# LSH attention with a fused feed-forward network: an add by transfer, features behind the product, an earlier load, one engine per last output

## The chip, the cores and the metric

The program runs on one core of one Trainium2 chip, in one launch. The metric is the device time of that launch in microseconds (us). The engines are TensorE (PE, matmuls and transposes), VectorE (DVE), ScalarE (ACT), GpSimd (POOL), and SyncE (SP), which here only issues transfers.

## The reference

Attention first: 4 batches, 8 heads, 768 tokens of 64 numbers. Each query and key is hashed to 6 bits, the signs of its products with a projection; a query sees only keys with equal bits. Then a feed-forward network (FFN) over all 3072 tokens.

```python
mask = q_bucket[:, :, :, None] == k_bucket[:, :, None, :]
scores = np.where(mask, scale * (q @ k.T), -1e9)       # per batch and head
attn = np.exp(scores - scores.max(-1, keepdims=True))
attn = attn / (attn.sum(-1, keepdims=True) + 1e-09)
x = (attn @ v).transpose(0, 2, 1, 3).reshape(B * S, H * D)   # 3072 x 512
h = x @ w_in                                           # 512 -> 2048
g = h * np.clip(h + 3.0, 0.0, 6.0) / 6.0
out = g @ w_out                                        # 2048 -> 512
```

## The kernel before

All inputs and outputs are fp32; a matrix product is done as three matmuls of numbers split in a high and a low half (names with h and l at the end: xh, xl, gh, gl, ph, pl). ScalarE makes most high halves by a cast, DVE or POOL the low ones by a subtraction.

**Attention** is a loop over 192 steps k, one for each 128 queries of a head: the transposes pt of the weights (L351), the accumulation acc of the values (L388, L389; 12 matmuls in every second step, for 256 queries), the scores s of a later step (L319, L322). DVE takes the minimum (L329) and makes pl (L375), ScalarE the exponential (L341) and ph (L374). ScalarE copies a finished acc to y (L416). One half of its partitions holds the product of the high values, the other that of the low ones. SP stores the one half in an HBM buffer xs, and POOL adds the other there by an accumulating transfer (`add()`, L395), one of 512 columns and one of 256 for every head. In the last head of a batch (`last_head`) DVE adds the two halves instead (L413, L414), and SP's store is enough.

**FFN.** Batch 0's FFN runs in the middle, after step 52. Those of batches 1 to 3 are a generator, `ffn()`, which the attention loop resumes twice per step, so that its matmuls lie between those of the attention; when the attention is over, it runs on alone. It works on chunks of 256 tokens, three per batch, called the first to the ninth here (h1_0 to h3_2), and in each on 16 blocks fc of 128 hidden features: gemm1 (12 matmuls into h, L494 to L496), a yield, gemm2 of the block before (6 matmuls into po, L516 to L518), the gate (ScalarE L503, DVE L504, gh, and gl on POOL, L509), a yield.

**Features of the next chunk** are made on the side. `begin()` loads xr from xs and puts small jobs in a list `side`: some empty ones, one that inverts the sums (L434, L435), one that spreads them to a tile rb (L442, POOL), and one for each of four feature blocks that transposes rb to rt on PE (L452), multiplies it in on DVE (L455) and spreads the next. `beside()` takes one job off the list. It is called once behind the gate and once more after the yield, just before the next gemm1. When the list is empty, `split()` makes xh on ScalarE (L485), and xl on DVE for feature blocks 0 and 2, on POOL for 1 and 3 (L486). In the last batch tiles of the tags kk and qq take their place.

**Order.** The instruction order of PE, DVE, ScalarE and POOL is that of the program text; each engine runs its own list in order. `bank()` hands out four PSUM banks, two of each of the tags pt and pu, which alternate: pt, acc, rt and h all come from it. SP and POOL issue their transfers in order.

Of the kernel before, what the change touches and what calls it, by code (L numbers as in the profile page):

```python
# [33 lines left out]
WA = 4  # L34
WB = 5
XE = 8
XF = (9, 8)
NWARM = 30


# [1 line left out]
def lsh_attention_moe(  # L42
# [10 lines left out]
    nc = tc.nc  # L53
    B, H, D, S = qkT.shape
    D //= 2
    DM, DF = w_in.shape
# [17 lines left out]
    def dma(out: bass.AP, in_: bass.AP):  # L74
        nonlocal last
        last = nc.sync.dma_start(out=out, in_=in_)
# [3 lines left out]
    def bank(shape, name: str, tag: str | None = None):  # L80

        nonlocal turn
        if tag is None:
            tag = ("pt", "pu")[turn % 2]
            turn += 1
        return ps.tile(shape, F32, name=name, tag=tag, bufs=2)
# [311 lines left out]
    def output(un: int):  # L398
        nonlocal vdone
        i, u = divmod(un, KT // 2)  # L400
        b, h = divmod(i, H)
        o = (h % 2) * D
        acc = accs.pop(un)

        if u != 1:
            outs[i] = sp.tile([P, 4 * P if u == 0 else 2 * P], F32, name=f"y{i}_{u}", tag=f"y{u}", bufs=1)
        y = outs[i][:, 2 * P :] if u == 1 else outs[i][:, : 2 * P]

        r = slice(o, o + D)
        r2 = slice(D - o, 2 * D - o)  # L410
        last_head = h == H - 1
        if last_head:
            nc.scalar.copy(y[r], acc[r2])  # L413
            nc.vector.tensor_add(y[r], acc[r], y[r])  # L414
        else:
            nc.scalar.copy(y, acc[:])  # L416
        if u:
            c = slice(0, 4 * P) if u == 1 else slice(4 * P, S)
            to = xs[b][h * D : (h + 1) * D, c]

            with tc.issue_after(copied.ins):
                dma(out=to, in_=outs[i][r])
            if not last_head:
                adds.append((i, to, outs[i][r2]))
        vdone = 2 * un + 2
# [31 lines left out]
    def load_x(b: int, t: int, ccs: range):  # L457
        assert all(not b * H <= a[0] < b * H + ccs.stop * P // D for a in adds)
        ts = slice(t * TC, (t + 1) * TC)
        xr = sp.tile([P, NCC, TC], F32, name=f"xr{b}_{t}", tag="ob")  # L460
        dma(
            out=xr[:, : len(ccs)], in_=xs[b][: len(ccs) * P, ts].rearrange("(cc p) t -> p cc t", p=P)
        )
        return xr

    def scale_x(b: int, t: int, ccs: range, xr, rc=None):

        name = f"{b}_{t}"
        rbs = {}

        def invert():
            rbs["rc"] = rc if rc is not None else inverse(name, b, slice(t * TC, (t + 1) * TC), ccs)

        def spread_next(cc: int):
            if cc < len(ccs):
                rbs[cc] = spread(name, rbs["rc"], cc)

        def then(cc: int):
            normalise(f"{name}_{cc}", xr[:, cc], rbs.pop(cc), "pt" if ffn_on and b == 0 else None)
            spread_next(cc + 1)  # L480

        return [invert, lambda: spread_next(0)] + [lambda cc=cc: then(cc) for cc in ccs]

    def split_x(x, src, engine):
        nc.scalar.copy(x[0], src)  # L485
        engine.tensor_sub(x[1], src, x[0].bitcast(F32))  # L486

    def gemm1(n: str, fc: int, x, tag: str | None = None):
        hp = bank([P, TC], f"h{n}_{fc}", tag)
        wi = wt[2 * fc]  # L490
        for cc in range(NCC):
            xh, xl = x[cc]
            wc = slice(cc * P, (cc + 1) * P)
            nc.tensor.matmul(hp[:], lhsT=wi[:, 0, wc], rhs=xh, start=(cc == 0), stop=False)  # L494
            nc.tensor.matmul(hp[:], lhsT=wi[:, 0, wc], rhs=xl, start=False, stop=False)  # L495
            nc.tensor.matmul(hp[:], lhsT=wi[:, 1, wc], rhs=xh, start=False, stop=(cc == NCC - 1))  # L496
        return hp
# [22 lines left out]
    def store(b: int, t: int, po, end: bool = False):  # L520
        ob = sp.tile([P, TC // P, DM], F32, name=f"ob{b}_{t}", tag="ob")
        r0 = b * S + t * TC
        to = out[r0 : r0 + TC, :].rearrange("(u p) d -> p u d", p=P)
        for u in range(TC // P):
            if end:

                x = DM // 2
                nc.scalar.mul(ob[:, u, :x], po[u][:, :x], 1.0 / 6.0)
                nc.vector.tensor_scalar_mul(ob[:, u, x:], po[u][:, x:], 1.0 / 6.0)
                dma(out=to[:, u], in_=ob[:, u])  # L530
            else:
                nc.scalar.mul(ob[:, u], po[u], 1.0 / 6.0)
        if not end:
            dma(out=to, in_=ob[:])
# [4 lines left out]
    side = []  # L539

    def beside():
        if side:
            side.pop(0)()
# [185 lines left out]
    def ffn():  # L729
        nonlocal ffn_on  # L730
        chunks = [(b, t) for b in range(1, B) for t in range(NTC)]
        xr, xhl = {}, {}
        pend = None

        def there(c: int) -> bool:

            return vdone >= (chunks[c][0] + 1) * HK

        def begin(c: int):
            b, t = chunks[c]  # L740
            xr[c] = load_x(b, t, range(NCC))
            todo = scale_x(b, t, range(NCC), xr[c])
            if b < B - 1:
                side.extend([lambda: None] * 2 + todo)
                return

            side.extend([lambda: None] * (4 if t else 6) + todo[:2])
            for cc in range(NCC):
                side.append(todo[2 + cc])
                side.append(lambda cc=cc: (place(c) if cc == 0 else None, split(c, cc)))  # L750

        def place(c: int):
            b, t = chunks[c]
            n = f"{b}_{t}"
            if b == B - 1 and t % 2 == 0:
                h, l = (
                    sp.tile([P, 2 * S], F32R, name=f"{x}{n}", tag=x)[:, : NCC * TC] for x in ("kk", "qq")
                )
                h, l = (x.rearrange("p (cc t) -> p cc t", cc=NCC) for x in (h, l))
            else:  # L760
                h, l = (sp.tile([P, NCC, TC], F32R, name=f"{x}{n}", tag=x, bufs=1) for x in ("xh", "xl"))
            xhl[c] = [(h[:, cc], l[:, cc]) for cc in range(NCC)]

        def split(c: int, cc: int):
            split_x(xhl[c][cc], xr[c][:, cc], (nc.vector, nc.gpsimd)[cc % 2])

        def finish():
            nonlocal pend
            which, (fc, po, gh, gl) = pend
            gemm2(fc, po, gh, gl)  # L770
            pend = None
            if fc + 1 < NFC:
                return lambda: None
            return lambda: store(*which, po, which == chunks[-1])

        for c, (b, t) in enumerate(chunks):
            while not there(c):
                if pend is not None:
                    finish()()
                yield  # L780
            n = f"{b}_{t}"
            if c not in xr:
                begin(c)
            while side:
                beside()
                yield
                yield
            if c not in xhl:
                place(c)
                for cc in range(NCC):  # L790
                    split(c, cc)
            ffn_on = True
            copy, engine = (nc.scalar.copy, nc.vector) if b == B - 1 else (nc.vector.tensor_copy, nc.gpsimd)
            po = None
            for fc in range(NFC):
                hp = gemm1(n, fc, xhl[c])
                yield
                end = finish() if pend is not None else lambda: None
                if po is None:
                    po = ps.tile([P, 2, 512], F32, name=f"po{n}", tag="s" if b == B - 1 and t % 2 == 0 else "po", bufs=1)  # L800
                gg = gate(n, fc, hp, copy, engine)
                end()
                pend = ((b, t), (fc, [po[:, u] for u in range(2)], *gg))
                if c + 1 < len(chunks) and c + 1 not in xr and there(c + 1):
                    if fc >= XF[chunks[c + 1][0] == B - 1]:
                        begin(c + 1)
                if fc + 1 == NFC and c + 1 in xr and c + 1 not in xhl and not side:
                    place(c + 1)
                    for cc in range(NCC):
                        split(c + 1, cc)  # L810
                else:
                    beside()
                yield
                beside()
            del xhl[c]
        finish()()

# [182 lines left out]
```

## Time and profile before

| what | value |
|---|---|
| time, median of 3 runs | 1032.8 us (1032.73 to 1034.37) |
| profiled execution | 1033.77 us |
| its span, first to last instruction | 1031.6 us |
| TensorE clock granted, mean | 0.995 of full speed (the 2.4 GHz level) |
| busy: PE, DVE, ScalarE, POOL | 98%, 67%, 57%, 46% of the span |

The profile is that of one execution. Spans of matmuls overlap in it, since their ends are modelled; the distance from one start to the next tells more. In brackets behind a row of the timeline stands how long the engine was idle before it, and what released it.

### The profile page before, as it was taken

How to read it: one execution, taken by the hardware profiler on the slowest of the kernel's cores; microseconds unless marked ns; L12 is line 12 of the kernel's file. 1: busy time of each engine (PE TensorE's matmuls, PEld its weight loads, DVE VectorE, ACT ScalarE, POOL GpSimd, SP SyncE). 2: the span in 40 equal slices, each digit the busy share in tenths (PEclk: the TensorE clock that was granted, in tenths of full speed). 3: DMA queues.
4: the chain of work that ended last, by engine and by line, in shares of the span. 5: the costliest groups of instructions: out<-in, count | busy, mean ns of one | idle time of the engine just before them, and what ended most of it. 6: DMA issues, size and time to landing. Idle time of an engine off the chain costs nothing.

```text
span 1031.6 us, 19001 instructions
## 1 busy us (share of the span) xinstructions
PE 1007.9 (98%) x6846; PEld 925.8 (90%) x6846; DVE 688.2 (67%) x1445; ACT 585.2 (57%) x1311; POOL 470.4 (46%) x522
## 2 busy tenths in 40 slices
PE   8999989999999999999999999999999999999998
PEld 7999878888899998898999999999999999899996
DVE  6999988889579999656556666655656553333332
ACT  6889865555488887544544554554455452333332
POOL 5677625566357775634553534553544232200100
PEclk9999999999999999999999999999999999999999
DMA  3566669000145555322321322221232010101000
GB/s 102 149 139 178 169 213 352 2 1 1 26 135 114 119 125 133 69 62 52 95 48 40 84 71 56 64 77 41 63 95 44 20 32 29 42 1 42 1 22 20
DMA packets 47412, 80.68 MB, mean 78 GB/s; under 512 B 5924, under 2 KB 27812, under 8 KB 47320
## 3 DMA queue, kind: packets, MB, share of 16 engines
q1 hardware_dynamic: 42840, 73.98, 24.5%
q0 software_dynamic: 4480, 5.51, 4.8%
q8 instruction: 54, 0.88, 0.4%
q14 instruction: 38, 0.31, 0.1%
HBM read 41.95 MB, written 18.09 MB: 58 GB/s over the span
## 4 chain that ended last, share of the span: by engine, by line
PE 80%; DVE 12%; ACT 3%; issue 3%; DMA 1%; POOL 0%; DVEq 0%; POOLq 0%; ACTq 0%
PE pt L351 10%; PE h L495 7%; PE h L494 7%; PE h L496 7%; PE po L516 7%; PE po L518 7%; PE po L517 7%; PE acc L388 6%; PE acc L389 6%; PE s L319 5%; PE s L322 5%; DVE pl L375 2%; DVE p L329 2%; DVE qq L290 1%; PE z L281 1%
## 5 line engine op out<-in xcount | busy, mean ns | idle before, releaser
L329 DVE TENSOR_SCALAR_CACHE_REDUCE p<-s 128x768 f32<-128x768 f32 x192 | 183.5, 955 | 99.8 <-PE pt L351 95.4
L375 DVE TENSOR_TENSOR pl<-pt,ph 128x384 fp32r<-128x384 f32 x376 | 191.7, 550 | 50.7 <-ACT ph L374 48.9
L374 ACT CAST ph<-pt 128x384 fp32r<-128x384 f32 x376 | 165.5, 481 | 53.4 <-PE pt L351 42.6
L341 ACT ACTIVATE p<-p,m 128x768 f32<-128x768 f32 x192 | 179.6, 935 | 9.3 <-DVE p L329 8.8
L503 ACT ACTIVATE g<-h,three 128x256 f32<-128x256 f32 x192 | 91.4, 476 | 153.5 <-PE h L496 129.5
L351 PE MATMUL pt<-ident,p 128*128 128x128 f32 x1152 | 161.5, 274 | 7.3 <-DVE pl L375 5.7
L509 POOL TENSOR_TENSOR gl<-g,gh 128x256 fp32r<-128x256 f32 x96 | 74.4, 775 | 202.9 <-DVE gh L508 159.8
L351 PEld LDWEIGHTS pt<-ident,p 128*128 128x128 f32 x1152 | 136.5, 141 | 25.6 <-PE pt L351 4.0
L504 DVE SCALAR_TENSOR_TENSOR g<-g,h 128x256 f32<-128x256 f32 x192 | 80.5, 419 | 114.1 <-ACT g L503 111.7
L388 PE MATMUL acc<-ph,vv 128*128 128x256 f32 x564 | 152.6, 303 | 3.1 <-DVE pl L375 3.1
L494 PE MATMUL h<-xh,w 128*128 128x256 f32 x512 | 147.8, 289 | 1.2 <-ACT y L416 1.2
L495 PE MATMUL h<-xl,w 128*128 128x256 f32 x512 | 143.3, 280 | 0.1
L496 PE MATMUL h<-xh,w 128*128 128x256 f32 x512 | 143.2, 280 | 0.0
L389 PE MATMUL acc<-pl,vv 128*128 128x256 f32 x564 | 141.0, 283 | 0.0
L516 PE MATMUL po<-w,gh 128*128 128x512 f32 x320 | 126.7, 396 | 0.1
L518 PE MATMUL po<-w,gl 128*128 128x512 f32 x320 | 126.6, 395 | 0.0
L517 PE MATMUL po<-w,gh 128*128 128x512 f32 x320 | 126.2, 394 | 0.0
L388 PEld LDWEIGHTS acc<-ph,vv 128*128 128x128 f32 x564 | 107.3, 190 | 6.2 <-DVE pl L375 1.9
L389 PEld LDWEIGHTS acc<-pl,vv 128*128 128x128 f32 x564 | 107.8, 191 | 0.0
L319 PE MATMUL s<-kk,qq 76*128 76x384 f32 x384 | 101.6, 345 | 2.2 <-ACT kk L295 1.5
L322 PE MATMUL s<-kk,qq 128*128 128x384 f32 x384 | 100.6, 343 | 0.0
L494 PEld LDWEIGHTS h<-xh,w 128*128 128x128 f32 x512 | 96.4, 188 | 3.8 <-ACT y L416 2.4
(136 smaller groups left out, 2019.3 us busy)
## 6 DMA issues: line engine op xcount, KB each, us to landing
raw<-in_qkT SPq DMA_DIRECT2D x32, 384.0 KB, 3.5
kk<-qq SPq DMA_DIRECT2D x62, 192.0 KB, 3.2
wr<-in_w_in SPq DMA_DIRECT2D x16, 512.0 KB, 9.7
wr<-in_w_out SPq DMA_DIRECT2D x16, 512.0 KB
vr<-in_v SPq DMA_DIRECT2D x32, 192.0 KB, 2.8
qq<-qq SPq DMA_DIRECT2D x31, 192.0 KB, 3.6
out<-ob SPq DMA_DIRECT2D x11, 512.0 KB, 3.0
xr<-xs SPq DMA_DIRECT2D x9, 512.0 KB
```

The source lines that it names most:

```text
L329: nc.vector.tensor_scalar(out=pr_[:], in0=s[:, :, :HW], scalar1=CAP, scalar2=None, op0=ALU.min, op1=ALU.min, accum_out=m[:],)
L341: nc.scalar.activation(pr_[:], pr_[:], AF.Exp, bias=m[:], scale=-1.0, accum_out=sms[b][:, t, h : h + 1])
L351: nc.tensor.transpose(pt[:, x], probs[g][0][:, c, x * P : (x + 1) * P], ident[:])
L375: nc.vector.tensor_sub(lo[:, :, w], pt[:], hi[:, :, w].bitcast(F32))
L388: nc.tensor.matmul(acc[:], lhsT=vv[:, kt], rhs=hi[:, x], start=(kt == 0), stop=False)
L389: nc.tensor.matmul(acc[:], lhsT=vv[:, kt], rhs=lo[:, x], start=False, stop=(kt == KT - 1))
L494: nc.tensor.matmul(hp[:], lhsT=wi[:, 0, wc], rhs=xh, start=(cc == 0), stop=False)
L495: nc.tensor.matmul(hp[:], lhsT=wi[:, 0, wc], rhs=xl, start=False, stop=False)
L496: nc.tensor.matmul(hp[:], lhsT=wi[:, 1, wc], rhs=xh, start=False, stop=(cc == NCC - 1))
L516: nc.tensor.matmul(po[u], lhsT=gh[:, us], rhs=wo[:, 0], start=(fc == 0), stop=False)
L517: nc.tensor.matmul(po[u], lhsT=gh[:, us], rhs=wo[:, 1], start=False, stop=False)
L518: nc.tensor.matmul(po[u], lhsT=gl[:, us], rhs=wo[:, 0], start=False, stop=(fc == NFC - 1))
```

## The change

Five edits. In batch 1, the last head's first 512 columns are stored and added by transfer as in other heads, and only its last 256 are added on DVE. The chunks of the last batch are begun from block fc 7 on instead of 8. The list of the first chunk has three empty jobs instead of two. The second call of `beside()` stands directly behind gemm1 instead of before the next one, and not in block 0. Of the last output, ScalarE scales all 512 columns for the first 128 tokens and DVE all 512 for the others, where each did half of both.

```diff
@@ -34,7 +34,7 @@
 WA = 4
 WB = 5
 XE = 8
-XF = (9, 8)
+XF = (9, 7)
 NWARM = 30
 
 
@@ -408,7 +408,8 @@
 
         r = slice(o, o + D)
         r2 = slice(D - o, 2 * D - o)
-        last_head = h == H - 1
+
+        last_head = h == H - 1 and (b != 1 or u == 2)
         if last_head:
             nc.scalar.copy(y[r], acc[r2])
             nc.vector.tensor_add(y[r], acc[r], y[r])
@@ -524,9 +525,10 @@
         for u in range(TC // P):
             if end:
 
-                x = DM // 2
-                nc.scalar.mul(ob[:, u, :x], po[u][:, :x], 1.0 / 6.0)
-                nc.vector.tensor_scalar_mul(ob[:, u, x:], po[u][:, x:], 1.0 / 6.0)
+                if u == 0:
+                    nc.scalar.mul(ob[:, u], po[u], 1.0 / 6.0)
+                else:
+                    nc.vector.tensor_scalar_mul(ob[:, u], po[u], 1.0 / 6.0)
                 dma(out=to[:, u], in_=ob[:, u])
             else:
                 nc.scalar.mul(ob[:, u], po[u], 1.0 / 6.0)
@@ -741,7 +743,7 @@
             xr[c] = load_x(b, t, range(NCC))
             todo = scale_x(b, t, range(NCC), xr[c])
             if b < B - 1:
-                side.extend([lambda: None] * 2 + todo)
+                side.extend([lambda: None] * (2 if c else 3) + todo)
                 return
 
             side.extend([lambda: None] * (4 if t else 6) + todo[:2])
@@ -794,6 +796,8 @@
             po = None
             for fc in range(NFC):
                 hp = gemm1(n, fc, xhl[c])
+                if fc:
+                    beside()
                 yield
                 end = finish() if pend is not None else lambda: None
                 if po is None:
@@ -811,7 +815,6 @@
                 else:
                     beside()
                 yield
-                beside()
             del xhl[c]
         finish()()
 
```

How the edits move instructions is shown in three places. On PE, in block 12 of the first chunk (h1_0), where a feature block of the second chunk (rt1_1) is made, before:

```order
L388 MATMUL acc58_6490<-ph58_1_6395,vv19_6216 128x256
L389 MATMUL acc58_6490<-pl58_1_6396,vv19_6216 128x256
L452 MATMUL rt1_1_1_6503<-ident_69,rb1_1_1_6476 128x128 x2
L494 MATMUL h1_0_12_6509<-xh1_0_5751,w24_3160 128x256
L495 MATMUL h1_0_12_6509<-xl1_0_5752,w24_3160 128x256
L496 MATMUL h1_0_12_6509<-xh1_0_5751,w24_3160 128x256
```

and now:

```order
L497 MATMUL h1_0_12_6530<-xh1_0_5778,w24_3160 128x256
L495 MATMUL h1_0_12_6530<-xh1_0_5778,w24_3160 128x256
L496 MATMUL h1_0_12_6530<-xl1_0_5779,w24_3160 128x256
L497 MATMUL h1_0_12_6530<-xh1_0_5778,w24_3160 128x256
L453 MATMUL rt1_1_1_6543<-ident_69,rb1_1_1_6516 128x128 x2
L279 MATMUL z21_6553<-qq_21_6411,pjl_74 108x384
```

The rt stood between acc and h. Now it follows the 12 matmuls of h and stands ahead of the hash z; and since the FFN is a step later against the attention, this h comes behind pt, not behind acc.

On POOL, at the start of the first chunk (gl1_0_0 belongs to its first block; qq_19 and kk_19 to a head of the attention; xs2 is the buffer of batch 2), before:

```order
L442 COPY rb1_0_3_5676<-rc1_0_5507 128x256
L266 CAST qq_19_5710<-raw19_5561 128x768
L271 TENSOR_TENSOR kk_19_5709<-raw19_5561,qq_19_5710 64x768
L272 TENSOR_TENSOR qq_19_5710<-raw19_5561,qq_19_5710 64x768
L486 TENSOR_TENSOR xl1_0_5752<-xr1_0_5436,xh1_0_5751 128x256 x2
L395 DMA xs2_127<-y17_0_5678 64x512
L509 TENSOR_TENSOR gl1_0_0_5793<-g1_0_0_5791,gh1_0_0_5792 128x256
```

and now:

```order
L443 COPY rb1_0_2_5669<-rc1_0_5537 128x256
L443 COPY rb1_0_3_5702<-rc1_0_5537 128x256
L266 CAST qq_19_5705<-raw19_5558 128x768
L271 TENSOR_TENSOR kk_19_5704<-raw19_5558,qq_19_5705 64x768
L272 TENSOR_TENSOR qq_19_5705<-raw19_5558,qq_19_5705 64x768
L395 DMA xs2_127<-y17_0_5671 64x512
L487 TENSOR_TENSOR xl1_0_5779<-xr1_0_5435,xh1_0_5778 128x256 x2
L510 TENSOR_TENSOR gl1_0_0_5817<-g1_0_0_5815,gh1_0_0_5816 128x256
```

The transfer that adds y17_0 stood behind the two subtractions xl1_0 of the first chunk, and now stands ahead of them.

On POOL, at the start of the fourth chunk (xl2_0), before:

```order
L509 TENSOR_TENSOR gl1_2_14_8726<-g1_2_14_8724,gh1_2_14_8725 128x256
L271 TENSOR_TENSOR kk_27_8756<-raw27_8524,qq_27_8757 64x768
L272 TENSOR_TENSOR qq_27_8757<-raw27_8524,qq_27_8757 64x768
L509 TENSOR_TENSOR gl1_2_15_8781<-g1_2_15_8779,gh1_2_15_8780 128x256
L486 TENSOR_TENSOR xl2_0_8787<-xr2_0_8390,xh2_0_8786 128x256 x2
L395 DMA xs3_128<-y25_0_8703 64x512
L509 TENSOR_TENSOR gl2_0_0_8859<-g2_0_0_8857,gh2_0_0_8858 128x256
```

and now:

```order
L271 TENSOR_TENSOR kk_27_8729<-raw27_8489,qq_27_8730 64x768
L272 TENSOR_TENSOR qq_27_8730<-raw27_8489,qq_27_8730 64x768
L510 TENSOR_TENSOR gl1_2_14_8754<-g1_2_14_8752,gh1_2_14_8753 128x256
L395 DMA xs3_128<-y25_0_8676 64x512
L510 TENSOR_TENSOR gl1_2_15_8821<-g1_2_15_8819,gh1_2_15_8820 128x256
L487 TENSOR_TENSOR xl2_0_8827<-xr2_0_8430,xh2_0_8826 128x256 x2
L510 TENSOR_TENSOR gl2_0_0_8883<-g2_0_0_8881,gh2_0_0_8882 128x256
```

Here the transfer of y25_0 has moved ahead of gl of the third chunk's last block and of both xl.

## Rows read from the trace of the kernel before

**Rows 1.** The page, part 1: busy time, share and count of each engine.
```profile
PE 1007.9 (98%) x6846; PEld 925.8 (90%) x6846; DVE 688.2 (67%) x1445; ACT 585.2 (57%) x1311; POOL 470.4 (46%) x522
```

**Rows 2.** Waits of PE, 395 to 1032 us: total us, times, longest.
```profile
PE h L494 <- ACT y L416: 1.2, 5, 0.2
...
PE rt L452 <- POOL rb L442: 0.5, 2, 0.3
PE h L495 <- POOL qq L486: 0.4, 1, 0.4
```

**Rows 3.** Timeline of PE, 480 us: start, length, operation, idle before and releaser.
```profile
480.08 0.38 PE L452 MATMUL rt<-ident,rb 128*128 128x128 f32 x2
480.70 0.39 PE L494 MATMUL h<-xh,w 128*128 128x256 f32 x1 [0.24 <-ACT y L416]
480.93 0.28 PE L495 MATMUL h<-xl,w 128*128 128x256 f32 x1
```

**Rows 4.** Timeline of PE, 887 to 890 us.
```profile
887.57 0.38 PE L452 MATMUL rt<-ident,rb 128*128 128x128 f32 x2
887.70 0.37 PE L494 MATMUL h<-kk,w 128*128 128x256 f32 x1
...
888.90 0.38 PE L494 MATMUL h<-kk,w 128*128 128x256 f32 x1
889.70 0.38 PE L495 MATMUL h<-qq,w 128*128 128x256 f32 x1 [0.42 <-POOL qq L486]
```

**Rows 5.** Timeline of PE, one cycle, and the fourth chunk's first matmul.
```profile
657.37 0.28 PE L494 MATMUL h<-xh,w 128*128 128x256 f32 x1
...
658.77 0.52 PE L319 MATMUL s<-kk,qq 76*128 76x384 f32 x2
...
661.45 0.36 PE L494 MATMUL h<-xh,w 128*128 128x256 f32 x1
...
667.13 0.28 PE L494 MATMUL h<-xh,w 128*128 128x256 f32 x1
```

**Rows 6.** Timeline of DVE and PE in batch 1's last head.
```profile
384.56 0.43 DVE L414 TENSOR_TENSOR y<-acc,y 64x256 f32<-64x256 f32 x1
...
384.68 0.52 PE L351 MATMUL pt<-ident,p 128*128 128x128 f32 x3 [0.32 <-DVE pl L375]
```

**Rows 7.** Timeline of POOL at the place of the new transfer.
```profile
393.82 2.14 POOL L242 TENSOR_SCALAR raw<-raw 64x768 f32<-64x768 f32 x1 [4.67 <-DMA raw<-in_qkT]
```

**Rows 8.** Timeline of POOL and DVE around two inversions (L434).
```profile
400.33 1.84 POOL L272 TENSOR_TENSOR qq<-raw,qq 64x768 fp32r<-64x768 f32 x1
...
401.20 1.00 DVE L434 TENSOR_SCALAR rc<-sms 128x16 f32<-128x16 f32 x1
...
556.27 0.17 DVE L434 TENSOR_SCALAR rc<-sms 128x16 f32<-128x16 f32 x1
```

**Rows 9.** Timeline of ScalarE and DVE at the end.
```profile
1026.60 0.38 ACT L528 ACTIVATE ob<-po 128x256 f32<-128x256 f32 x1 [1.81 <-PE po L518]
...
1027.89 0.42 DVE L529 TENSOR_SCALAR ob<-po 128x256 f32<-128x256 f32 x1 [0.45 <-ACT ob L528]
```

**Rows 10.** Timeline of POOL and SP at the first chunk's start.
```profile
419.72 1.68 POOL L486 TENSOR_TENSOR xl<-xr,xh 128x256 fp32r<-128x256 f32 x2
...
420.18 0.46 SPq L76 DMA_DIRECT2D xs<-y  x1
...
422.95 0.90 POOL L395 DMA_DIRECT2D xs<-y  x1 [1.54 <-ACT g L503]
```

**Rows 11.** Timeline of PE, first and last matmul of the first chunk's first h.
```profile
419.57 0.28 PE L494 MATMUL h<-xh,w 128*128 128x256 f32 x1
...
421.69 0.28 PE L496 MATMUL h<-xh,w 128*128 128x256 f32 x1
```

**Rows 12.** Timeline of POOL at the fourth chunk's start.
```profile
670.50 0.89 POOL L395 DMA_DIRECT2D xs<-y  x1 [2.80 <-DVE gh L508]
```

**Rows 13.** The page, part 5: POOL's gl; count, busy us, mean ns, idle before.
```profile
L509 POOL TENSOR_TENSOR gl<-g,gh 128x256 fp32r<-128x256 f32 x96 | 74.4, 775 | 202.9 <-DVE gh L508 159.8
```

## The prediction

> **What bounds the kernel now.** The page comes first: TensorE (PE) is busy for 1007.9 of 1031.6 us, while the next engine, VectorE (DVE), has 67% [rows 1]. No part of the change takes a matmul away, so all it can win or lose is the roughly 24 us in which PE does nothing or starts late. The waits of PE after 395 us, where batches 1 to 3 run, come second [rows 2]. They are small: five waits of h for the copy y, two of rt for the spread factors rb, one of h for the low half qq. These idle times are lower bounds, because the shown end of a matmul is modelled (0.28 us long, though the next one starts 0.12 us after it), so I read the distance from start to start in the timeline instead.
>
> **What goes.** (1) At each of the five chunk changes between 480 and 813 us the last rt stands between acc and h, and h starts 0.62 us after rt, waiting for the copy y (L416) of the acc just finished [rows 3]. After another rt, where nothing waits, h starts 0.13 us later [rows 4]. So 0.49 us is lost; the matmul behind it starts 0.23 us after h where 0.12 is usual (12 of them in the 1.40 us of an undisturbed h, [rows 5]), another 0.11. The new order puts rt behind h, and by the first two pieces of order h then follows acc or pt directly, as in the run of fc blocks in which PE does not wait. Five times 0.60 is -3.0. (2) The two rt that wait for rb [rows 2] go too: idle 0.5 in all, with the late restart -0.6. (3) At 888.90 us the first block after the attention waits for the last low half qq: the next matmul starts 0.80 us later instead of 0.12, then 0.1 more [rows 4]. With features begun at fc 7 instead of 8 the half is made a block (about 2.8 us) earlier: -0.8. (4) Two of the three adds on DVE (L414) of batch 1's last head go. Each took 0.43 us, in a stretch where DVE sets the pace (PE then waited 0.32 us shown) [rows 6]: -0.9, bounds -0.6 and -1.0. ScalarE's copy keeps its 256 columns and does more partitions, for which I count nothing. The transfer that replaces the adds is issued by POOL at about 393 us, where POOL waits 4.67 us for a load of raw anyway [rows 7]: covered. (5) The add of 1e-9 (L434) took 1.00 us at 401.20 and 0.17 at 556.27; it ended when POOL's qq (L272) ended at 402.17, in the same DVE-paced stretch [rows 8]. The change puts it one step, some 2 us, later, when that instruction is over. I take -0.6, bounds 0 and -0.85.
>
> The Trainium skill (SBUF — State Buffer, section SBUF: two separate sides) says that DVE and GpSimd share a port pair which is locked for a whole instruction, the other engine being blocked. By it the invert costs 0.17 where POOL is idle and up to the rest of POOL's instruction where not, so the same 1.00 us could come back at the new place; the sum would be 0.6 higher then. The trace agrees at 401.20.
>
> (6) The end: ScalarE and DVE take halves by turns from 1026.60 until 1028.31 [rows 9]. Afterwards ScalarE does 512 columns of u=0, and then DVE 512 of u=1. Those widths cost between once and twice the rows' 0.38 and 0.42; I take 0.6 and 0.75, nearer to twice: -0.3, bounds 0 and -0.8. Sum of what goes: -3.0 - 0.6 - 0.8 - 0.9 - 0.6 - 0.3 = -6.2.
>
> **What comes.** (7) Three empty slots instead of two start the FFN of batch 1 one step later. One more step runs without FFN work under it, and is then paced by DVE: +0.2 (0 to 0.33, the wait of such a step in [rows 6]). The fc block that moves behind the attention costs nothing, since PE is full there. The larger effect is that the parity turns: the first h of every chunk now follows a pt, and the previous acc is half a cycle older. On POOL, which works in order, the transfer add of the head (L395) then stands ahead of the low halves xl (L486) in two places [both POOL pieces of order]. POOL blocks at such an add until SP's store has landed.
>
> At the first chunk, acc ends and h starts at T = 419.57; the store is issued at 420.18 and the add begins at 422.95, T+3.4, and takes 0.90 [rows 10]. Two xl took 1.68 [rows 10], so the first is ready at T+5.1, the second at T+6.0. On PE, rt, s and pt come before h, some 1.5 us, and the low half of feature block 1 is wanted 0.5 us into h: T+2.1. So h would stand 3.0 us, and 0.1 again at block 3. Now it loses 2.24 - 1.40 = 0.84: 419.57 to 421.69 plus one spacing [rows 11], against 1.40 [rows 5]. Net +2.3.
>
> At the fourth chunk (batch 2), T is 667.13 [rows 5]. The add begins at 670.50, T+3.4, and ends at T+4.3 [rows 12]; gl, now behind it, takes 0.78 [rows 13], the two xl 0.84 each: T+5.9 and T+6.8. PE first has h of fc 15, s, po and pt, 4.08 us from 657.37 to 661.45 [rows 5], then wants block 1 at T+4.6: 1.3 us stand, and 0.2 at block 3, +1.5. The other four chunk starts have gl and xl without an add just ahead: +0.3 together. Two or three rt come to wait behind a blocked POOL by up to 0.3 each, as the two rows now do [rows 2]: +0.3. Sum of what comes: 0.2 + 2.3 + 1.5 + 0.3 + 0.3 = +4.6.
>
> A rule bears on this price. The Trainium skill (DMA: Bandwidth & Descriptors, section Anatomy of one DMA — SWDGE (gpsimd) path) fits 2.0 us plus bytes over 436 GB/s, most of it the receipt of the write; for this 64x512 store an estimate from it is 2.3 us. The trace has 2.77 from the store's issue to the add, and I use that. By the rule both stalls would be 0.5 shorter, the time 1030.2.
>
> **Sum.** -6.2 + 4.6 = -1.6. The profiled execution took 1033.77 us, 2.2 of it outside the span, so 1032.2 by its own time; it is one of the slower ones, the median of the runs being 1032.8 (1032.73 to 1034.37). From the median: 1031.2.
>
> **Rivals.** A: the adds don't hold the low halves up, because POOL's wait is short or xl is not on the path. For it: xl also waits for ScalarE's xh and DVE does half of them. Against: the add at 422.95 began 1.5 us after POOL had finished all before it, so it does wait. Then +2.3 and +1.5 vanish: 1027.4.
> B (slower): the blocked POOL reaches all chunk starts. If in the other four POOL's add or casts also put xl 1.5 us behind, as at the fourth chunk, that is +5.7 more instead of 0.3: 1036.9. It decides once late low halves cost over 6.2 us in all, against the 4.1 I count. Against it: in those four the order has the add behind xl or a step earlier.
> C: the waits at the chunk changes stay, because h then waits for another bank or for the features that are made later: without term 1, 1034.2. For it: the banks turn in the same way, and rt still takes one.
>
> **Chances.** Forecast 1031.2 with its own range 1029.6 to 1032.7: 0.57. A 0.21, C 0.12, B 0.10. This kernel's measurement can tell about 0.2%, 2.1 us, from no change: faster is under 1030.7, slower over 1034.9. A and a third of the forecast's case make faster 0.40; B and the upper part of C make slower 0.13; same 0.47. The range for all: 1027.2, just under A, to 1034.3, just over C; B and the tails are left out, near 0.2.
>
> **What would show it.** Right: no h waiting for y at the five chunk changes; no rt of 0.3 us waiting at 485 and 734; in the first chunk's first h one L495-type matmul (xl) waiting about 3 us for POOL's xl, and the same with 1.3 us near 670; the add starting 2.8 us after its store; the two PE waits at 384 and 389 gone; L434 of the first chunk at 0.2 us; the last DVE instruction ending near 1.5 us after PE. Wrong: no wait at these two first h (A), such waits at other chunk starts too (B), or h still waiting at the chunk changes (C).

## Result and profile after

The changed kernel takes 1036.88 us (median of 6 runs, 1035.23 to 1038.71), the kernel before 1032.93 (6 runs, 1032.73 to 1034.37). The ratio is 1.0034, 95% interval 1.0023 to 1.0044: slower by 3.5 us by that ratio, where 1.6 us faster was forecast, and outside the range of 1027.2 to 1034.3. The profiled execution took 1035.23 us, with a span of 1033.2; it is the fastest of the six.

First the waits of PE behind 395 us, which answer to [rows 2] (total us, times, longest):

```profile
PE h L496 <- POOL xl L487: 2.2, 2, 1.2
PE s L319 <- DVE qq L290: 1.2, 1, 1.2
PE rt L453 <- POOL rb L443: 1.1, 1, 1.1
PE h L495 <- ACT xh L486: 0.9, 1, 0.9
PE rt L453 <- DVE pl L375: 0.8, 2, 0.6
PE z L280 <- DMA kk<-qq: 0.7, 1, 0.7
PE acc L388 <- DVE pl L375: 0.7, 2, 0.4
PE po L519 <- POOL gl L510: 0.5, 2, 0.3
PE z L281 <- POOL rb L443: 0.3, 1, 0.3
PE h L496 <- DVE xl L487: 0.3, 1, 0.3
```

The five waits of h for y are gone, and so are the one for qq and the long wait of pt for pl. In their place stand more waits than there were before, and other ones. The largest group belongs to one place, the first h of the first chunk, with three waits in h and one of s behind it. These four in the timeline of PE (start, length, idle before and releaser), where the rows of [rows 11] have none in brackets:

```profile
419.56 0.39 PE L495 MATMUL h<-xh,w 128*128 128x256 f32 x1 [0.87 <-ACT xh L486]
...
420.23 0.39 PE L496 MATMUL h<-xl,w 128*128 128x256 f32 x1 [0.29 <-DVE xl L487]
...
422.06 0.39 PE L496 MATMUL h<-xl,w 128*128 128x256 f32 x1 [1.21 <-POOL xl L487]
...
425.55 0.62 PE L319 MATMUL s<-kk,qq 76*128 76x384 f32 x2 [1.24 <-DVE qq L290]
```

By the start-to-start distance to the usual spacing they cost 1.1, 0.6, 1.4 and 1.4 us, 4.4 together, where the kernel before lost 0.84 in this h. The engines that release them, at the same place (SP and POOL answer to [rows 10]):

```profile
417.56 0.46 SPq L76 DMA_DIRECT2D xs<-y  x1
...
419.10 1.32 ACT L486 CAST xh<-xr 128x256 fp32r<-128x256 f32 x4
...
420.31 0.90 POOL L395 DMA_DIRECT2D xs<-y  x1 [1.86 <-DVE xl L487]
421.29 1.41 POOL L487 TENSOR_TENSOR xl<-xr,xh 128x256 fp32r<-128x256 f32 x2
...
424.41 1.09 DVE L290 TENSOR_SCALAR qq<-z,thr,val 44x768 fp32r<-44x768 f32 x1 [2.55 <-PE z L281]
```

The transfer stands ahead of xl, and POOL is idle for 1.86 us until the store has landed, 2.75 us after its issue. (The row names DVE's xl as the releaser, which the transfer doesn't need; at the fourth chunk, in both kernels, the transfer begins 2.76 and 2.77 us after its store with other engines named.) That was forecast. Not forecast: ScalarE begins the four xh only at 419.10, so that even the first matmul waits; and the hash z, which in the new order comes right behind this first h, is followed at once by the scores s, which need the bits that DVE makes from z (L290). Before, z followed the second h and had the six matmuls of gemm2 between it and s; block 0 has no gemm2 yet.

The fourth chunk, PE and POOL (answers to [rows 12]):

```profile
669.18 0.90 POOL L395 DMA_DIRECT2D xs<-y  x1 [3.80 <-ACT xh L486]
669.84 1.02 POOL L510 TENSOR_TENSOR gl<-g,gh 128x256 fp32r<-128x256 f32 x1
670.53 1.69 POOL L487 TENSOR_TENSOR xl<-xr,xh 128x256 fp32r<-128x256 f32 x2
...
671.59 0.39 PE L496 MATMUL h<-xl,w 128*128 128x256 f32 x1 [0.98 <-POOL xl L487]
```

Here the forecast's queue is seen as it was drawn, add, gl, xl; it costs 1.1 us. The same queue makes rb late at 485 us:

```profile
483.40 0.90 POOL L395 DMA_DIRECT2D xs<-y  x1 [5.71 <-ACT ph L374]
484.06 1.01 POOL L510 TENSOR_TENSOR gl<-g,gh 128x256 fp32r<-128x256 f32 x1
484.74 0.67 POOL L443 COPY rb<-rc 128x256 f32<-128x256 f32 x1
...
485.46 0.44 PE L453 MATMUL rt<-ident,rb 128*128 128x128 f32 x2 [1.12 <-POOL rb L443]
```

The order add, gl, rb is that of the kernel before. But this add begins 4.4 us after its store, which SP issued at 478.99; in the kernel before it begins 2.9 us after (480.68 to 483.60). Why the store takes longer here isn't shown. The two waits of po for a late gl, at 518 and 767 us, come from adds that stand ahead of gl and wait for their stores longer still. SP and POOL ahead of the first of these waits, before and then now:

```profile
512.77 0.46 SPq L76 DMA_DIRECT2D xs<-y  x1
513.33 0.53 SPq L76 DMA_DIRECT2D raw<-in_qkT  x1
...
515.56 0.90 POOL L395 DMA_DIRECT2D xs<-y  x1 [2.02 <-ACT p L341]
```

```profile
510.60 0.33 SPq L76 DMA_DIRECT2D raw<-in_qkT  x1
...
511.94 0.47 SPq L76 DMA_DIRECT2D xs<-y  x1
...
517.12 0.89 POOL L395 DMA_DIRECT2D xs<-y  x1 [5.73 <-DVE p L329]
```

With the turn by a step SP issues the load of raw (384 KB) ahead of the store instead of behind it, and the add begins 5.2 us after its store instead of 2.8. At 765 us it is the same, 5.2 against 2.8. That the load is what delays the store is argued from this order; no run changes the order alone.

Ahead of the FFN, the inversion has become shorter, but PE waits at the next instruction instead (answers to [rows 8]):

```profile
399.45 1.00 POOL L306 TENSOR_TENSOR vv<-vr,vv 128x384 fp32r<-128x384 f32 x1
...
399.97 0.51 DVE L435 TENSOR_SCALAR rc<-sms 128x16 f32<-128x16 f32 x1
...
400.64 0.40 PE L280 MATMUL z<-kk,pjh 128*108 128x384 f32 x1 [0.70 <-DMA kk<-qq]
...
401.34 0.41 PE L281 MATMUL z<-qq,pjh 128*108 128x384 f32 x1 [0.31 <-POOL rb L443]
```

z needs the rows of kk and qq that SP copies (the second row names rb, which z doesn't read; in a second profile of the changed kernel the copy of qq stands there). Start to start it now waits 0.86 and 0.53 us. L435 ended at 400.48, when POOL's subtraction vv (L306) ended, at 400.45.

The end, ScalarE and DVE (answers to [rows 9]):

```profile
1027.73 0.60 ACT L529 ACTIVATE ob<-po 128x512 f32<-128x512 f32 x1 [1.81 <-PE po L519]
...
1028.36 0.69 DVE L531 TENSOR_SCALAR ob<-po 128x512 f32<-128x512 f32 x1 [1.99 <-ACT ob L529]
```

DVE is done 1.32 us after ScalarE's start, where it was 1.71.

A comparison of the two profiles alone would mislead. In that of the kernel before PE's granted clock is at the 1.2 GHz level for part of two stretches that the change doesn't touch; in the profile of the changed kernel it isn't. PE in windows (us, busy, clock, share of DMA, GB/s), before and then after:

```profile
10.00:15.00 5.00, 4.62 (x17) 0.66 0.61 189
140.00:145.00 5.00, 4.95 (x27) 0.66 0.74 201
```

```profile
10.00:15.00 5.00, 4.21 (x22) 1.00 0.63 175
140.00:145.00 5.00, 4.06 (x31) 1.00 0.88 278
```

At 305 us, ahead of every edit, the changed kernel is 2.3 us early by this alone; its last matmul is 1.1 us late (1027.24 against 1026.11). So the edits cost some 3.4 us between the two profiles.

### The profile page after: what moved, and what is told of

The parts are those of the page before. It is cut to its first block, busy times and chain, and to the rows that moved or that the text cites. A ratio compares the mean times of both kernels' runs of the same rounds, so it can differ in the third digit from the quotient of the medians.

```text
span 1033.2 us, 19004 instructions
## 1 busy us (share of the span) xinstructions
PE 1006.2 (97%) x6846; PEld 924.7 (90%) x6846; DVE 687.7 (67%) x1442; ACT 584.9 (57%) x1310; POOL 470.1 (46%) x523
## 4 chain that ended last, share of the span: by engine, by line
PE 80%; DVE 11%; ACT 3%; issue 3%; DMA 1%; POOL 1%; SPq 0%; DVEq 0%; POOLq 0%; ACTq 0%
PE pt L351 10%; PE h L496 7%; PE h L497 7%; PE h L495 7%; PE po L519 7%; PE po L517 7%; PE po L518 7%; PE acc L388 6%; PE acc L389 6%; PE s L319 5%; PE s L322 5%; DVE p L329 2%; DVE pl L375 2%; DVE qq L290 1%; DVE wr L183 1%
## 5 line engine op out<-in xcount | busy, mean ns | idle before, releaser
L496 PEld LDWEIGHTS h<-xl,w 128*128 128x128 f32 x512 | 96.5, 188 | 5.2 <-POOL xl L487 3.3
L417 ACT COPY y<-acc 128x256 f32<-128x256 f32 x86 | 32.1, 373 | 120.8 <-PE acc L389 116.2
```

## Experiments

Two theories at the start. P: the third empty job costs, because the FFN turns by one step against the attention. Q: the new transfer of batch 1's last head costs, since SP and POOL are held up. The phase of the two loops that two empty jobs give is called the even one, that of three the odd one.

**Two empty jobs again.** The changed kernel, with:

```diff
-                side.extend([lambda: None] * (2 if c else 3) + todo)
+                side.extend([lambda: None] * 2 + todo)
```

> The changed kernel with two empty jobs again in the first chunk's list; the other edits stay. Theory P (the third empty job turns the FFN by one step against the attention, so that POOL's transfer adds stand ahead of the low halves xl at the first and fourth chunk, and the hash z directly ahead of s at the first): the waits of PE at these two starts (1.1 + 0.6 + 1.4 + 1.4 us at the first, 1.1 at the fourth) and the two late gl (0.4 and 0.5) go, and the time is 1030 to 1031.5. Rival Q (the new transfer of batch 1's last head holds up SP and POOL and is what costs): within 1 us of the changed kernel, 1036 to 1037.

Measured 1028.57 us against 1032.99 for the kernel before on the same chip: ratio 0.9958 (0.9945 to 0.9971). Of PE's waits behind 395 us these are left:

```profile
PE pt L351 <- DVE pl L375: 1.0, 1, 1.0
PE acc L388 <- DVE pl L375: 0.8, 2, 0.4
```

Both were there in the kernel before; of the other waits of the section above none is left, with the transfer of the last head still in. That is P, and the time lies 1.4 us below P's range: the wait of rt for rb (1.3) and the two of z (1.4), which P had not named, go too. The wait of pt is that for the inversion, which takes 0.98 us again.

**Three empty jobs alone.** The kernel before, with:

```diff
-                side.extend([lambda: None] * 2 + todo)
+                side.extend([lambda: None] * (2 if c else 3) + todo)
```

> The kernel before with three empty jobs instead of two in the first chunk's list, and nothing else. Theory P: slower, 1035 to 1038, with the same waits at the first and fourth chunk as in the changed kernel. Rival Q: no difference, 1032.5 to 1033.5. Theory R (the turn by a step alone also takes away the five waits of h for y): those five, 0.6 each, are gone in its trace.

Measured 1044.18 us, ratio 1.0111 (1.0092 to 1.0129): even more than P said. The first h of the first chunk waits as in the changed kernel, to 0.01 us (0.86, 0.29, 1.21, 1.24 idle), and so does that of the fourth (0.99). Some of PE's other waits:

```profile
PE rt L452 <- POOL rb L442: 1.8, 2, 0.9
...
PE h L494 <- ACT y L416: 1.1, 5, 0.2
...
PE h L495 <- POOL qq L486: 0.4, 1, 0.4
```

So the turn by a step doesn't take the five waits for y away (theory R falls); moving rt behind h does. Its profiled execution took 1039.8 us; the other five 1043.2 to 1047.7, with mean clocks of 0.991 to 0.996 against 0.998. They have no trace, so where they lost these 3.4 to 7.9 us isn't shown. The next experiment moves rt alone.

**beside() behind gemm1 alone.** The kernel before, with:

```diff
                 hp = gemm1(n, fc, xhl[c])
+                if fc:
+                    beside()
                 yield
...
                 yield
-                beside()
```

> The kernel before with the second call of beside() behind gemm1 and nothing else. Theory P: the five waits of h for y go, 3.0 us, and nothing takes their place: 1029 to 1030.5. Theory Q: the same. Rival S (rt behind gemm1 waits for rb, which POOL makes late, as the 1.1 us wait of an rt for rb in the changed kernel at 485 us): 1031.5 to 1033.

Measured 1030.23 us, ratio 0.9973 (0.9964 to 0.9981), 2.8 us faster. The five waits for y and the two for rb are gone from its trace. One has come, against P: at 419.92 the first h waits 0.7 us idle for DVE's xl. S falls: with the old phase no rt waits for rb.

**The add by transfer alone.** The kernel before, with:

```diff
-        last_head = h == H - 1
+        last_head = h == H - 1 and (b != 1 or u == 2)
```

> The kernel before with batch 1's last head added by transfer for its first 512 columns and nothing else. Theory P: two adds on DVE go (1.0 us); the later load of the first chunk is hidden: 1031.5 to 1032.5. Rival Q: z waits for the copies of kk, which SP issues behind that load: slower, 1034 to 1036.

Measured 1032.04 us, ratio 0.9991 (0.9982 to 0.9999), some 1 us faster. The two waits that [rows 6] stand for have gone; a wait of z for the copies of qq has come, 0.2 us idle. Q falls.

**The adds behind xl.** The changed kernel, its odd phase kept, with the transfers of y17_0 and y25_0 issued a step later, so that on POOL they come behind the low halves at the first and fourth chunk:

```diff
-        if t in (1, 4):
+        if t in ((2, 4) if i in (18, 26) else (1, 4)):
             add()
```

> The changed kernel with two transfer adds (of y17_0 and y25_0) issued one step later, so that on POOL they stand behind the low halves xl of the first and the fourth chunk; all else as in the changed kernel. Theory P1 (what the turn by a step costs is POOL's blocking at these adds, as predicted): the waits of h for xl at both places go, 1.4 and 1.1 us, and with them most of the loss: 1031 to 1033. Theory P2 (the adds are only a part; at the first chunk h also waits for xh, 1.1, and s for the bits of z, 1.4, because the first h now has nothing of the FFN behind it): the two xl waits go and the others stay: 1034 to 1035.5.

Measured 1033.94 us, ratio 1.0011 to the kernel before (1.0002 to 1.0019). The waits for POOL's xl are gone from its trace; the largest of the others are there (its first three rows):

```profile
PE s L319 <- DVE qq L290: 1.2, 1, 1.2
PE rt L453 <- POOL rb L443: 1.0, 1, 1.0
PE h L495 <- ACT xh L486: 0.9, 1, 0.9
```

That is P2, at the lower edge of its range. The queue on POOL at these two places, on which the prediction rested, is real and worth some 2.4 us of the changed kernel's time (1.0034 against 1.0011). Without it the odd phase still stands some 5.5 us above the even one (1.0011 against 0.9958). What makes up these 5.5 us is read from the waits in the traces; no run takes away one of them alone. Adds ahead of rb and gl, as at 485 and 517 us, are still among them.

**Four empty jobs.** The changed kernel, with 4 in place of 3:

```diff
-                side.extend([lambda: None] * (2 if c else 3) + todo)
+                side.extend([lambda: None] * (2 if c else 4) + todo)
```

> The changed kernel with four empty jobs in the first chunk's list. Theory P (it is the odd turn against the attention, h behind pt and z directly behind the first h, that costs, not the later start): as with two, 1027.5 to 1030. Rival L (each step by which the FFN starts later costs): slower than the changed kernel, 1037 or more.

Measured 1028.19 us, ratio 0.9956 (0.9942 to 0.9970). Two steps later is as fast as none; it is the odd step that costs, not the lateness. L falls.

**The old end.** The changed kernel with two empty jobs, and the last output halved as before:

```diff
-                if u == 0:
-                    nc.scalar.mul(ob[:, u], po[u], 1.0 / 6.0)
-                else:
-                    nc.vector.tensor_scalar_mul(ob[:, u], po[u], 1.0 / 6.0)
+                x = DM // 2
+                nc.scalar.mul(ob[:, u, :x], po[u][:, :x], 1.0 / 6.0)
+                nc.vector.tensor_scalar_mul(ob[:, u, x:], po[u][:, x:], 1.0 / 6.0)
```

> The changed kernel with two empty jobs, and the last output halved between ScalarE and DVE for each 128 tokens as before. From the two traces (from PE's last matmul to the end of the span 5.49 us before, 5.96 after) the old end is 0.5 us shorter, because its first store leaves 0.4 us earlier relative to the last matmul: 1028.1 against 1028.6 with the new end. By the prediction's step the new end is 0.3 shorter: 1028.9.

Measured 1027.57 us, ratio 0.9957 (0.9945 to 0.9970): the interval is that of the new end, so the times don't tell the two apart. The traces do. From the start of PE's last matmul to the end of the span it is 5.48 to 5.52 us in the five profiles with the old end, and 5.08 to 5.16 in four with the new one. In the fifth, the changed kernel's own, it is 5.96, since there the last store took 0.85 us longer behind DVE's end than in all others. What I expected of this run rested on that one profile and was wrong; the prediction's -0.3 stands.

**The changed kernel again, for its clock.** No edit.

> The changed kernel once more, for a second profile. If TensorE's clock is what puts the median of its runs (1036.9, mean clock 0.995) above its profiled run (1035.2, 0.999), a run of 1036 to 1038 shows a stretch at the lower level within 60 us behind the waits at 419 to 427 us. If not, the low stretches lie only in the first 150 us, as in the kernel before.

This execution took 1038.18 us. PE in windows of it, as above:

```profile
420.00:425.00 5.00, 3.38 (x14) 0.68 0.50 105
425.00:430.00 5.00, 3.76 (x14) 0.50 0.04 11
430.00:435.00 5.00, 5.00 (x33) 0.79 0.19 54
```

The same windows of the first profile of the changed kernel:

```profile
420.00:425.00 5.00, 2.87 (x17) 1.00 0.39 93
425.00:430.00 5.00, 4.45 (x35) 1.00 0.13 26
430.00:435.00 5.00, 5.00 (x35) 1.00 0.24 52
```

The granted clock falls to the 1.2 GHz level (0.50) while PE stands in the waits of the first h, and comes back some 10 us later. From the first matmul of that h to the first of block 4 it took 26.4 us here, 22.7 in the first profile, and 20.1 in the kernel before. So the waits behind this first matmul cost 2.6 us by themselves, and 3.7 more when the clock falls with them. That it fell here is shown in this execution alone. Of the first six, four had mean clocks of 0.993 to 0.995, while of 38 runs of the kernel before beside the experiments 2 had 0.995 and the others more. That suggests the same fall in them, but a mean doesn't say where the clock was low: the kernel with four empty jobs has 0.994 in its profile, with low stretches before 150 us alone.

## Why the prediction was wrong

The step that failed is (7), the price of the third empty job, with the rt waits summed beside it. Its mechanism, an add on POOL that waits for a store and makes the low halves late, was right at the two places named. But the list of what depends on the phase was too short, and the wait from a store to its add was taken as the same everywhere.

- (7) as a whole: with the other four edits kept, the third job was forecast to cost 4.6 less the 0.6 of (5), 4.0 us. Between the ratios with three jobs and with two (1.0034 against 0.9958) it cost 7.9.
- (7), first chunk: +2.3 forecast. Measured 4.4 - 0.84 = +3.6 from wait to wait. Inside h the reckoning held: POOL's xl lets h go on at 422.06, 5.1 us after the end of acc as forecast, and the three waits up to there are 3.0 together, where 3.1 was forecast. But 1.7 of them pass in waits for xh and DVE's xl, which I had not counted, so POOL's add is worth only 1.4 here. What the term lacked is the 1.4 us of s behind z. No term held a fall of TensorE's clock in these waits either, 3.7 us in the execution that shows it.
- (7), fourth chunk: +1.5 forecast, 1.1 measured. The other four: +0.3 forecast, and each waits 0.15 at a first xl, 0.6.
- Waits of rt for rb: +0.3 forecast. One of 1.3 us came, at 485, behind an add that begins 4.4 us after its store, where I had taken 2.77 everywhere; in the kernel with the third job alone two came, of nearly 1 us each, behind adds at the usual 2.8. I had taken over the size of the two waits before, which the turn by a step changes. Not forecast: two waits of po for a late gl, 0.4 and 0.5, behind adds 5.2 us after their stores.
- (1) -3.0 and (2) -0.6: right; the waits (1) names are gone here, and both kinds with beside() alone, whose gain of 2.8 us is about these terms less its new wait for DVE's xl.
- (3) -0.8: right by the trace; no h waits for qq in the changed kernel nor with two empty jobs, and one does in the three kernels with three jobs, beside() or the transfer alone, which begin the last chunks from block 8 on as before.
- (4) -0.9: right, some 1 us with the transfer alone. (6) -0.3: right in four of five profiles.
- (5) -0.6: the invert went from 1.00 to 0.51 us, not to 0.17, since another POOL instruction was under way. The Trainium skill (SBUF — State Buffer, section SBUF: two separate sides) had said that the port pair of the two engines is locked for a whole instruction, and L435's end with that of POOL's subtraction agrees. The gain was lost anyway: z, now 4.6 us behind SP's first copy of kk instead of 5.8, waits 1.4 us for these copies.

Summed from the traces up to PE's last matmul, the terms (1) to (4) won 5.4 us. Lost were 3.6 + 1.1 + 0.6 at the chunk starts, 1.3 + 0.9 in rt and po, 0.2 net in (5), and 0.6 by more waits of acc, pt and rt for DVE in the steps before the FFN, one more than before: 8.3. That is 2.9 of the 3.4 us between the profiles. Rivals A and C fall: the two first h wait, and no h waits for y at the chunk changes. Rival B, forecast at 1036.9 with a chance of 0.10, gave the time but not its way: POOL does not reach all chunk starts. Of the rule on transfers (the Trainium skill, DMA: Bandwidth & Descriptors, section Anatomy of one DMA — SWDGE (gpsimd) path), 2.3 us by estimate, the trace shows 2.75 again from the store to the add, and 4.4 and 5.2 at the places above. The section is on transfers that GpSimd issues, and this store is SP's, so the estimate was for another path.

The kernel with two empty jobs, that is four of the five edits, beats both: 1028.6 us, and 1027.6 with the old end, beside 1033.0 and 1032.3 for the kernel before on the same chips.

## What to carry to other kernels

Where two loops are interleaved by hand, shifting one by a step changes their phase everywhere: walk every dependency of the first block anew, on all engines, and that of whatever comes to stand next to it, not only the one that the shift was meant for. When an in-order engine both computes and issues transfers that wait for a store, as POOL does here, the store's landing stands ahead of its arithmetic; and how long a store takes, 2.8 to 5.2 us here for the same size, also turns with the phase. A stand of a few us on a busy TensorE may be paid twice, in itself and in the clock after it, as in one execution here; look at the mean clock of unprofiled runs too, and at more than one trace.

## Unexpected of the hardware

The clock's fall: in the changed kernel PE was busy for 16.4 of the 20 us from 400 to 420 in both profiled executions, and then stood in the same four waits. One lost the 2.4 GHz level, the other kept it (0.68, 0.50 and 0.79 against 1.00 in three windows of 5 us). The kernel with three jobs alone has these waits too and kept 1.00 in its one profile, and so did the one with the adds behind xl, with 3.1 us of waits there instead of 4.4. What decides is open.
